# A residual block with Winograd convolutions: weight blocks in natural tap order, one transposing DMA each, ordered by a copy that writes at a distance

## The chip, the core and the metric

The kernel runs on one core of a Trainium2 chip. The metric is the device time of one execution in microseconds (us), the median of several runs. Besides the times there is one execution recorded by the profiler, with every instruction of every engine: TensorE (PE, with its weight loads as PEld), VectorE (DVE), ScalarE (ACT), GpSimd (POOL) and SyncE (SP), which here only issues DMAs.

## What is computed

A residual block of a diffusion model, on x of 2 x 512 x 64 x 64 in bf16. Two times in a row: a group norm over 4 groups, silu, and a 3x3 convolution from 512 to 512 channels; between them a time embedding is added per channel, at the end the input.

```python
def conv3(z, w):
    zp = jnp.pad(z, ((0, 0), (0, 0), (1, 1), (1, 1)))
    taps = [jnp.einsum("bchw,oc->bohw", zp[:, :, i:i+H, j:j+W], w[:, :, i, j]) for i in range(3) for j in range(3)]
    ...
h = conv3(_silu(gn(x, g1, be1)), w1)
emb = _silu(t_emb) @ w_emb
h = h + emb.reshape(B, C, 1, 1)
h = conv3(_silu(gn(h, g2, be2)), w2)
return x + h
```

## The kernel before, in words

**Tiling.** Channels are cut into 4 tiles of 128. An image is cut into 2 chunks of 32 rows, so each layer (convolution) has 4 chunks: 2 images by 2. For each chunk and each tile `ot` of output channels, `one_set` runs a set of matmuls over the 4 tiles `ct` of input channels. The rows are convolved by Winograd's method with outputs in fours: six positions of transformed inputs V (made by `make_v` on DVE and ACT from the silu in `a_tmp`) meet six positions of transformed weights U. Some chunks (chunk 2 of layer 0, all of layer 1) use it along the columns too for the two outer positions, with weights that `u_cols` combines once more.

**The weights.** The transformed weights of one `ot` and `ct` come from one block of 128 x 1152 elements: 128 output channels by 128 input channels by 9 taps, as they lie in DRAM with the tap running fastest. PE needs them with input channels on the partitions, so each tap must be turned (128 x 128). For layer 0, `ot` 0 and 1 (8 blocks), PE turns them (`transposes`, line 348). The other 24 blocks (layer 0, `ot` 2 and 3; all 16 of layer 1) are built with `by_dma`, in `u_blocks` (line 427):

1. SP loads the block into one of two `stage` buffers (`u_load`, line 420).
2. ACT copies it in two instructions into nine dense slots of U (`order`): the six outer taps (ky 0 and 2), then the three middle ones (ky 1). It reads with a step of 9 elements and writes densely (lines 442 and 444).
3. Two transposing DMAs are issued on SP (`turn`, line 331): 768 columns into slots 0 to 5 of U, 384 columns into the scratch `g1t`.
4. ACT writes a quarter of the three taps of ky 0 into U and a half of the middle taps into `g1t` (lines 447 and 448).
5. DVE makes the four inner positions by six additions for a pair of blocks (lines 479 to 484); in layer 1, `u_cols` adds three more (lines 408 to 410).

U has 22 slots of 128 columns per block: before, 0 to 5 hold the outer taps (two by two), 8 to 19 the inner positions, 6, 7, 20 and 21 column combinations. A block of layer 1 goes into the place of the block of layer 0 with the same `ot` and `ct`, once the last chunk of layer 0 has used that one; so the 16 blocks of layer 1 are built during the last chunk of layer 0 and the first sets of layer 1, while the 8 of layer 0 are built during the first chunk.

**What sets the order.** No engine's order is written by hand. Every operation is given to a planner (`_Plan`, line 23) with its engine, a cost in us, what it reads and writes. `issue` (line 132) plays the list through with these costs and emits the instructions in the order found; a wrong cost gives a worse order, not a wrong program. `act` (line 296) gives a copy from SBUF 0.00084 us per element plus 0.09, whatever its step. `turn` gives a transposing DMA 0.42 us of SP. Each engine then works through its queue in order and waits where an operand isn't ready; so ACT's copies for the weights stand in one queue with the evacuations of PE's accumulators (`m<-acc`, `w<-acc`), the silus (`a_tmp`) and the scaled rows for V (`src<-vt`). SP's queue holds loads, stores and the transposing DMAs.

Of the kernel before, what the change touches and what calls it, by code (L numbers as in the profile page):

```python
# [10 lines left out]
ALU = mybir.AluOpType  # L11
AX = mybir.AxisListType
F32 = mybir.dt.float32
BF16 = mybir.dt.bfloat16
# [145 lines left out]
def kernel(  # L160
# [13 lines left out]
    nc = tc.nc  # L174
    P = nc.NUM_PARTITIONS
# [7 lines left out]
    NKX = 3  # L183
# [11 lines left out]
    NSL = 22  # L195
# [18 lines left out]
    plan = _Plan()  # L214
# [4 lines left out]
    def view(t, off, dims):  # L219
        base = t[:] if not isinstance(t, bass.AP) else t  # L220
        return bass.AP(base.tensor, base.offset + off, [list(base.ap[0])] + [list(d) for d in dims])
# [34 lines left out]
    def size(a):  # L256
        n = 1
        for d in list(a.ap)[1:]:
            n *= d[1]
        return n  # L260
# [16 lines left out]
    def tt(out, in0, in1, op, **kw):  # L277
        plan.add("DVE", vcost("tt", (out, in0, in1)),
                 lambda: nc.vector.tensor_tensor(out=out, in0=in0, in1=in1, op=op), [in0, in1], [out], **kw)  # L279

    def ts(out, in_, c, op=ALU.mult, c2=None, op1=None, more=(), **kw):
        def emit():
            if op1 is None:
                nc.vector.tensor_scalar(out=out, in0=in_, scalar1=c, scalar2=None, op0=op)  # L284
            else:
                nc.vector.tensor_scalar(out=out, in0=in_, scalar1=c, scalar2=c2, op0=op, op1=op1)
        plan.add("DVE", vcost("ts", (out, in_)), emit, [in_] + list(more), [out], **kw)
# [8 lines left out]
    def act(out, in_, func=None, scale=1.0, bias=None, accum=None, **kw):  # L296
        fn = func or ACT.Copy
        ps = in_.tensor.name in psum
        c = size(in_) * (0.00093 if fn == ACT.Silu else 0.00081 if ps else 0.00084) + 0.09
        if accum is not None:  # L300
            c += 0.08

        def emit():
            extra = {}
            if bias is not None:
                extra["bias"] = bias
            if accum is not None:
                extra["accum_out"] = accum
            nc.scalar.activation(out=out, in_=in_, func=fn, scale=scale, **extra)  # L309
        reads = [in_] + [a for a in (scale, bias) if a is not None and not isinstance(a, float)]  # L310
        plan.add("ACT", c, emit, reads, [out] + ([] if accum is None else [accum]), **kw)
# [18 lines left out]

    def turn(out, in_):
        n = 256 * size(out)
        plan.add("SP", 0.42, lambda: nc.sync.dma_start_transpose(out=out, in_=in_), [in_], [out], nbytes=1.5 * n)

    def pool(emit, reads, writes, cost=0.45, **kw):
        plan.add("POOL", cost, emit, reads, writes, **kw)
# [11 lines left out]
    def transposes(bank, pairs, tokens, reads, cost):  # L348
        def emit():
            t = bank.get()  # L350
            for sel, in_ in pairs:
                nc.tensor.transpose(sel(t), in_, ident[:in_.shape[0], :in_.shape[0]])
        plan.add("PE", cost, emit, reads + [ident[:]], tokens, lead=TURN, lat=0.2, wait=WAIT)
# [47 lines left out]
    def slots(U, c0, n, first, dims):  # L401
        return view(U, ((c0 % 2) * NSL + first) * P, [[NSL * P, n]] + dims)

    def u_cols(layer, ot, c0, n, tmp):
        U = u_pair(layer, ot, c0)
        two = lambda first: slots(U, c0, n, first, [[1, 2 * P]])
        ck = view(tmp, 0, [[2 * NKX * P, n], [1, 2 * P]])
        tt(ck, two(0), two(4), ALU.add)
        tt(two(6), ck, two(2), ALU.subtract)
        tt(two(20), ck, two(2), ALU.add)  # L410

    def u_more(layer, ot, c0, n):
        U = u_pair(layer, ot, c0)
        g = lambda kx: slots(U, c0, n, 8 + 4 * kx, [[2 * P, 2], [1, P]])
        ck = view(g1t, 0, [[2 * P, n], [P, 2], [1, P]])
        tt(ck, g(0), g(2), ALU.add)
        tt(slots(U, c0, n, 2, [[P, 2], [1, P]]), ck, g(1), ALU.subtract)
        tt(g(1), g(1), ck, ALU.add)

    def u_load(layer, ot, ct, **kw):  # L420
# [6 lines left out]
    def u_blocks(layer, ot, c0, loads, tmp=None, dve=False, act_scale=True, by_dma=False):  # L427
        n = len(loads)
        tmp = g1t if tmp is None else tmp
        U = u_pair(layer, ot, c0)  # L430
        taps = [[P, NKX], [1, P]]
        for i, wn in enumerate(loads):
            ct = c0 + i
            Ut[layer][ot][ct] = U[:, ct % 2]
            one = lambda first, step: slots(U, ct, 1, first, [[step * P, NKX], [1, P]])
            raw = slots(U, ct, 1, 0, [[1, 6 * P]])
            mid = [view(tmp, (2 * i + h) * NKX * P, [[1, NKX * P]]) for h in range(2)]
            wv = wn[:].rearrange("p (c ky kx) -> p kx ky c", ky=3, kx=3)
            if by_dma:
                order = view(U, ((ct % 2) * NSL + 8) * P, [[1, 9 * P]])  # L440
                flat = view(U, (ct % 2) * NSL * P, [[1, 6 * P]])
                act(order[:, 0:6 * P].rearrange("p (kx j c) -> p kx j c", j=2, c=P),
                    wn[:].rearrange("p (c ky kx) -> p kx ky c", ky=3, kx=3)[:, :, 0:3:2, :])
                act(order[:, 6 * P:9 * P].rearrange("p (kx c) -> p kx c", c=P), wv[:, :, 1, :])
                turn(flat.rearrange("p (k o) -> p k o", o=P), order[:, 0:6 * P])
                turn(mid[0].rearrange("p (k o) -> p k o", o=P), order[:, 6 * P:9 * P])
                act(one(11, 4)[:, 0], flat.rearrange("p (kx j o) -> p kx j o", j=2, o=P)[:, :, 0, :], scale=0.25)
                act(mid[1], mid[0], scale=0.5)
                continue
            pa, pb = XBank("xa", [NKX, 2, P], BF16), XBank("xb", [NKX, P], BF16)  # L450
            transposes(pa, [((lambda t, kx=kx, j=j: t[:, kx, j, :]), wv[:, kx, 2 * j, :])
                            for kx in range(NKX) for j in range(2)], ["xa"], [wn[:]], 0.45)
            transposes(pb, [((lambda t, kx=kx: t[:, kx, :]), wv[:, kx, 1, :]) for kx in range(NKX)],
                       ["xb"], [wn[:]], 0.23)

            def copy(out, bank, tok, size_, sel=lambda t: t[:], scale=None):
                if dve:
                    plan.add("DVE", 0.075 + size_ * 0.00052,
                             lambda: nc.vector.tensor_copy(out=out, in_=sel(bank.get())), [tok], [out])
                elif scale is None:  # L460
                    plan.add("ACT", 0.07 + size_ * 0.0008,
                             lambda: nc.scalar.copy(out=out, in_=sel(bank.get())), [tok], [out])
                else:
                    plan.add("ACT", 0.07 + size_ * 0.0008, lambda: nc.scalar.activation(
                        out=out, in_=sel(bank.get()), func=ACT.Copy, scale=scale), [tok], [out])

            copy(raw.rearrange("p a (k o) -> p (a k) o", o=P).rearrange("p (kx j) o -> p kx j o", j=2),
                 pa, "xa", 2 * NKX * P)
            copy(mid[0].rearrange("p (k o) -> p k o", o=P), pb, "xb", NKX * P)
            if act_scale and not dve:  # L470
                copy(one(11, 4)[:, 0], pa, "xa", NKX * P, lambda t: t[:, :, 0, :], 0.25)
                copy(mid[1].rearrange("p (k o) -> p k o", o=P), pb, "xb", NKX * P, scale=0.5)
        g = lambda j: slots(U, c0, n, j, [[2 * P, NKX], [1, P]])
        up = lambda j: slots(U, c0, n, 8 + j, [[4 * P, NKX], [1, P]])
        m = lambda h: view(tmp, h * NKX * P, [[2 * NKX * P, n], [P, NKX], [1, P]])
        if dve or not act_scale:
            ts(up(3), g(0), 0.25)
            ts(m(1), m(0), 0.5)
        tt(up(1), g(0), g(1), ALU.add)
        tt(up(0), up(1), m(0), ALU.add)  # L480
        tt(up(1), up(1), m(0), ALU.subtract)
        tt(up(3), up(3), g(1), ALU.add)
        tt(up(2), up(3), m(1), ALU.add)
        tt(up(3), up(3), m(1), ALU.subtract)
        if layer == 1:
            u_cols(layer, ot, c0, n, tmp)

    def u_tap(U, pos, kx):
        if pos in (0, NPOS - 1):
            return U[:, 2 * kx + (1 if pos else 0), :]  # L490
        return U[:, 8 + 4 * kx + pos - 1, :]

    def u_col(U, j, c):
        return U[:, (0, 20, 6, 4)[c] + j, :]

    def u_col_more(U, j, c):
        return U[:, (8 + 2 * j, 12 + 2 * j, 2 + j, 16 + 2 * j)[c], :]

    more_buf = lambda ct: (a_tmp + src)[ct]

# [317 lines left out]
    for i, prm in enumerate((g1, be1, g2, be2)):  # L818
        o = gparm[CT * i:CT * (i + 1), :]
# [156 lines left out]
```

## Time and profile before

| what | value |
|---|---|
| median of 3 runs | 536.96 us (536.06 to 537.66) |
| the profiled execution | 537.9 us |
| its span, first to last instruction | 536.1 us |
| mean granted clock of PE | 0.986 |
| busy: PE, DVE, ACT, POOL | 493.1, 463.5, 362.7, 35.3 us |
| ordering copies of the 24 blocks on ACT | 38.6 + 21.4 us |
| scaled copies of the 24 blocks on ACT | 11.6 + 11.6 us |
| DVE's additions of 768 elements on U | 28.5 us with `g1t` (x52), 15.5 us without (x28) |
| transposing DMAs on SP | 48, median 2.9 us from issue to landing |

How to read the views: a group of instructions is named by line, engine, operation and tiles, out<-in, with partitions x elements and a count; behind the bar stand the busy time, the mean time of one in ns, and the idle time of the engine just before them with what ended most of it. Since all DVE and ACT operations go through a few helpers, one line number (279 for two-operand additions, 309 for ACT) covers many tiles, and the tile names tell them apart. A row of the waits gives the waiting engine and tile, the engine and tile waited for, the total in us, how many times and the longest. A row of the stretches gives start:end, its length, the busy time of PE, PEld, DVE, ACT and POOL with their instructions, PE's granted clock, the mean busy share of the 16 DMA engines and GB/s. The rows for one tile give shortest/median/longest duration in ns, then the first and last start. The slices cut the span into 40 parts of 13.4 us, each digit a busy share in tenths.

### The profile page before, as it was taken

Reading aid. Unit: us, or ns where it says so; the run is one execution under the profiler, and the core shown is the slowest. Engines: PE = TensorE matmul, PEld = TensorE weight load, DVE = VectorE, ACT = ScalarE, POOL = GpSimd, SP = SyncE. Lnnn points to the kernel's source line nnn. Section 1 sums busy time; section 2 is a strip of 40 time slices with the busy share of each in tenths; the row PEclk is TensorE's granted clock in tenths of the full one; section 3 lists DMA queues with packets and bytes.
Section 4 is the critical chain, followed back from the end, with each engine's and each line's share of the span. In section 5 each row is a group of like instructions: output and inputs, shape, how many; then the busy total and the mean of one; then the engine's idle time right before and its main releaser. Section 6 shows DMA issues by size and latency. Waiting matters only on the chain. (4 is left out here: it accounts for less than half of the span.)

```text
span 536.1 us, 7685 instructions
## 1 busy us (share of the span) xinstructions
PE 493.1 (92%) x2769; PEld 262.4 (49%) x2770; DVE 463.5 (86%) x1048; ACT 362.7 (68%) x412; POOL 35.3 (7%) x83
## 2 busy tenths in 40 slices
PE   3889968989999999999996979997999999999994
PEld 3544423434444555554442435553555555566762
DVE  3989677998999997698867879997799999999966
ACT  4788999999966785569998897252645645323332
POOL 1210000001100200000000000003010000000010
PEclk9999999999999999999998889998999999999999
DMA  8302965562112313127677462525245354333444
GB/s 308 118 23 67 187 139 124 181 261 83 28 54 81 95 67 118 40 79 162 187 154 159 122 172 44 137 88 136 62 119 160 82 158 120 78 80 79 96 101 117
DMA packets 46496, 62.56 MB, mean 117 GB/s; under 512 B 31099, under 2 KB 32251, under 8 KB 45691
## 3 DMA queue, kind: packets, MB, share of 16 engines
q1 hardware_dynamic: 44096, 53.95, 34.0%
q0 software_dynamic: 2160, 7.87, 8.9%
q8 instruction: 21, 0.34, 0.3%
q10 hardware_dynamic: 203, 0.27, 0.1%
q14 instruction: 16, 0.13, 0.1%
HBM read 38.22 MB, written 16.78 MB: 103 GB/s over the span
## 5 line engine op out<-in xcount | busy, mean ns | idle before, releaser
L591 PE MATMUL acc<-V,U 128*128 128x512 bf16 (+1 forms) x2368 | 461.1, 355 | 21.4 <-DVE U L279 7.5
L591 PEld LDWEIGHTS <-U 128*128 128x128 bf16 x2496 | 243.6, 98 | 242.4 <-issue 22.1
L279 DVE TENSOR_TENSOR V<-vt 128x1056 bf16<-128x1056 bf16 (+2 forms) x124 | 84.1, 696 | 5.1 <-PE acc L591 2.1
L309 ACT ACTIVATE w<-acc 128x1024 bf16<-128x1024 f32 (+1 forms) x33 | 32.7, 990 | 41.7 <-PE acc L591 33.3
L309 ACT ACTIVATE U<-stage 128x768 bf16<-128x768 bf16 (+1 forms) x48 | 58.4, 1268 | 3.2 <-PE acc L591 1.8
L309 ACT ACTIVATE m<-acc 128x1024 bf16<-128x1024 f32 x28 | 28.4, 1014 | 39.8 <-PE acc L591 31.1
L309 ACT ACTIVATE a_tmp<-src,nb,sc 128x2112 bf16<-128x2112 bf16 x20 | 42.8, 2144 | 14.9 <-DMA src<-h_scr 5.4
L309 ACT ACTIVATE src<-vt 128x528 bf16<-128x528 bf16 x54 | 34.3, 635 | 26.7 <-DVE vt L279 26.7
L279 DVE TENSOR_TENSOR w<-m,w 128x1024 bf16<-128x1024 bf16 (+1 forms) x66 | 44.2, 670 | 8.7 <-ACT w L309 7.8
L279 DVE TENSOR_TENSOR U<-U,g1t 128x768 bf16<-128x768 bf16 (+2 forms) x76 | 37.0, 498 | 7.7 <-DMA g1t<-U 6.3
L279 DVE TENSOR_TENSOR vt<-a_tmp 128x1056 bf16<-128x1056 bf16 x52 | 36.6, 704 | 7.4 <-ACT a_tmp L309 6.5
L309 ACT ACTIVATE src<-V 128x2048 bf16<-128x2048 bf16 x16 | 30.5, 1905 | 0.3
L309 ACT ACTIVATE y<-y 128x2048 bf16<-128x2048 bf16 x16 | 30.4, 1897 | 0.0
L279 DVE TENSOR_TENSOR U<-U 128x768 bf16<-128x768 bf16 (+1 forms) x36 | 18.3, 509 | 12.5 <-ACT U L309 4.5
L309 ACT ACTIVATE a_tmp<-V,nb,sc 128x2112 bf16<-128x2112 bf16 x12 | 25.7, 2146 | 1.9 <-DVE nb L292 1.9
L309 ACT ACTIVATE mb<-acc 128x1024 bf16<-128x1024 f32 x20 | 20.4, 1020 | 9.1 <-PE acc L591 6.2
L526 POOL MEMSET a_tmp<- 128x64 bf16 x32 | 6.5, 208 | 280.5 <-DVE vt L279 153.8
L327 POOL DMA_DIRECT2D y<-in_x_dram x15 | 13.2, 879 | 154.0 <-DVE y L279 119.8
L279 DVE TENSOR_TENSOR vt<-vt,a_tmp 128x1056 bf16<-128x1056 bf16 x32 | 22.6, 706 | 0.6
L279 DVE TENSOR_TENSOR y<-sd,acc 128x512 bf16<-128x512 bf16 (+1 forms) x34 | 21.9, 686 | 0.8 <-PE acc L591 0.6
L279 DVE TENSOR_TENSOR w<-w 128x1024 bf16<-128x1024 bf16 x31 | 21.4, 689 | 0.6
L292 DVE SCALAR_TENSOR_TENSOR y<-w 128x512 bf16<-128x512 bf16 x32 | 21.0, 689 | 0.5
(110 smaller groups left out, 378.4 us busy)
## 6 DMA issues: line engine op xcount, KB each, us to landing
stage<-in_w_dram SPq DMA_DIRECT2D x32, 288.0 KB, 2.9
src<-h_scr SPq DMA_DIRECT2D x16, 528.0 KB, 3.8
h_scr<-y SPq DMA_DIRECT2D x16, 512.0 KB, 2.6
y<-in_x_dram POOLq DMA_DIRECT2D x15, 512.0 KB, 5.6
out_dram<-y SPq DMA_DIRECT2D x15, 512.0 KB, 2.7
V<-in_x_dram SPq DMA_DIRECT2D x6, 1024.0 KB, 7.4
src<-in_x_dram SPq DMA_DIRECT2D x4, 528.0 KB, 4.7
V<-in_x_dram SPq DMA_DIRECT2D x4, 512.0 KB, 6.8
```

The source lines that it names most:

```text
L279: lambda: nc.vector.tensor_tensor(out=out, in0=in0, in1=in1, op=op), [in0, in1], [out], **kw)
L292: nc.vector.scalar_tensor_tensor(out=out, in0=in0, scalar=scalar, in1=in1, op0=op0, op1=op1, **extra)
L309: nc.scalar.activation(out=out, in_=in_, func=fn, scale=scale, **extra)
L327: q.dma_start(out=out, in_=in_, **extra)
L526: pool(lambda r=r: nc.gpsimd.memset(rows[:, r, 1:W + 1], 0.0), [], [rows[:, r, 1:W + 1]], cost=0.2)
L591: nc.tensor.matmul(ap, lhsT=l, rhs=r, start=k == 0, stop=k == total[key] - 1)
```

## The change

The nine taps of a block are now kept in their natural order, ky before kx, in the slots of U, so that all nine can be turned at once. For the 24 blocks built by DMA:

- one ACT copy of 1152 elements takes the place of two; it reads the stage densely, as it lies, and writes the nine taps of a channel 128 elements (256 bytes) apart, into slots 9 to 17;
- one transposing DMA of 1152 columns takes the place of two; it writes slots 0 to 8, so the middle taps land in slots 3 to 5 of U and no longer in `g1t`;
- the scaled copies read from the new places; the half of the middle taps still goes to `g1t`.

For all 32 blocks the inner positions move from slots 8 to 19 to slots 9 to 20; the sum of the two outer taps is kept in `g1t` (or its stand-in) instead of in U; the column combinations go to slots 3, 4, 5 and 21, and their operands lie in two runs of 128 columns instead of one of 256. The addresses that PE and the PE-turned blocks use follow. The planner counts 1.25 us of SP for a transposing DMA instead of 0.42, and gets a higher cost for ACT copies that read SBUF with a last step above 4 elements. The new ordering copy has a last read step of 1, so it is counted at 0.00084 us per element, 1.06 us.

```diff
@@ act, turn
+        if not ps and list(in_.ap)[-1][0] > 4:
+            c = size(in_) * 0.00187 + 0.1
...
-        plan.add("SP", 0.42, lambda: nc.sync.dma_start_transpose(out=out, in_=in_), [in_], [out], nbytes=1.5 * n)
+        plan.add("SP", 1.25, lambda: nc.sync.dma_start_transpose(out=out, in_=in_), [in_], [out], nbytes=1.5 * n)
@@ u_cols
-        two = lambda first: slots(U, c0, n, first, [[1, 2 * P]])
-        ck = view(tmp, 0, [[2 * NKX * P, n], [1, 2 * P]])
-        tt(ck, two(0), two(4), ALU.add)
-        tt(two(6), ck, two(2), ALU.subtract)
-        tt(two(20), ck, two(2), ALU.add)
+        two = lambda first, step: slots(U, c0, n, first, [[step * P, 2], [1, P]])
+        ck = view(tmp, 0, [[2 * NKX * P, n], [P, 2], [1, P]])
+        tt(ck, two(0, 6), two(2, 6), ALU.add)
+        tt(two(3, 1), ck, two(1, 6), ALU.subtract)
+        tt(two(5, 16), ck, two(1, 6), ALU.add)
@@ u_blocks
+            fl = lambda first, dims: view(U, ((ct % 2) * NSL + first) * P, dims + [[1, P]])
+            outer, mids = fl(0, [[6 * P, 2], [P, NKX]]), fl(3, [[P, NKX]])
+            up3, half_mid = fl(12, [[4 * P, NKX]]), view(tmp, (2 * i + 1) * NKX * P, [[P, NKX], [1, P]])
+            if by_dma:
+                order, taps9 = fl(9, [[P, 9]]), fl(0, [[P, 9]])
+                act(order.rearrange("p k c -> p c k"), wn[:].rearrange("p (c k) -> p c k", k=9))
+                turn(taps9, order.rearrange("p k c -> p (k c)"))
+                act(up3, fl(0, [[P, NKX]]), scale=0.25)
+                act(half_mid, mids, scale=0.5)
+                continue
-            if by_dma:
-                order = view(U, ((ct % 2) * NSL + 8) * P, [[1, 9 * P]])
-                flat = view(U, (ct % 2) * NSL * P, [[1, 6 * P]])
-                act(order[:, 0:6 * P].rearrange("p (kx j c) -> p kx j c", j=2, c=P),
-                    wn[:].rearrange("p (c ky kx) -> p kx ky c", ky=3, kx=3)[:, :, 0:3:2, :])
-                act(order[:, 6 * P:9 * P].rearrange("p (kx c) -> p kx c", c=P), wv[:, :, 1, :])
-                turn(flat.rearrange("p (k o) -> p k o", o=P), order[:, 0:6 * P])
-                turn(mid[0].rearrange("p (k o) -> p k o", o=P), order[:, 6 * P:9 * P])
-                act(one(11, 4)[:, 0], flat.rearrange("p (kx j o) -> p kx j o", j=2, o=P)[:, :, 0, :], scale=0.25)
-                act(mid[1], mid[0], scale=0.5)
-                continue
...
-        tt(up(1), g(0), g(1), ALU.add)
-        tt(up(0), up(1), m(0), ALU.add)
-        tt(up(1), up(1), m(0), ALU.subtract)
+        tt(t(0), g(0), g(1), ALU.add)
+        tt(up(0), t(0), mid, ALU.add)
+        tt(up(1), t(0), mid, ALU.subtract)
         tt(up(3), up(3), g(1), ALU.add)
-        tt(up(2), up(3), m(1), ALU.add)
-        tt(up(3), up(3), m(1), ALU.subtract)
+        tt(up(2), up(3), t(1), ALU.add)
+        tt(up(3), up(3), t(1), ALU.subtract)
@@ u_tap
-            return U[:, 2 * kx + (1 if pos else 0), :]
-        return U[:, 8 + 4 * kx + pos - 1, :]
+            return U[:, (6 if pos else 0) + kx, :]
+        return U[:, 9 + 4 * kx + pos - 1, :]
```

Left out here: the same renumbering in `u_more`, `u_col` and `u_col_more`, and the copies of the PE-turned blocks into the new slots.

More of the change, by code (lines that the diff above doesn't have):

```diff
@@ L405, in u_cols @@
         U = u_pair(layer, ot, c0)
-        two = lambda first: slots(U, c0, n, first, [[1, 2 * P]])
-        ck = view(tmp, 0, [[2 * NKX * P, n], [1, 2 * P]])
-        tt(ck, two(0), two(4), ALU.add)
-        tt(two(6), ck, two(2), ALU.subtract)
-        tt(two(20), ck, two(2), ALU.add)
+        two = lambda first, step: slots(U, c0, n, first, [[step * P, 2], [1, P]])
[3 more added lines that the diff above has]
+        tt(two(5, 16), ck, two(1, 6), ALU.add)
     def u_more(layer, ot, c0, n):
         U = u_pair(layer, ot, c0)
-        g = lambda kx: slots(U, c0, n, 8 + 4 * kx, [[2 * P, 2], [1, P]])
+        g = lambda kx: slots(U, c0, n, 9 + 4 * kx, [[2 * P, 2], [1, P]])
         ck = view(g1t, 0, [[2 * P, n], [P, 2], [1, P]])
         tt(ck, g(0), g(2), ALU.add)
-        tt(slots(U, c0, n, 2, [[P, 2], [1, P]]), ck, g(1), ALU.subtract)
+        tt(slots(U, c0, n, 1, [[6 * P, 2], [1, P]]), ck, g(1), ALU.subtract)
         tt(g(1), g(1), ck, ALU.add)
@@ L434, in u_blocks @@
             Ut[layer][ot][ct] = U[:, ct % 2]
-            one = lambda first, step: slots(U, ct, 1, first, [[step * P, NKX], [1, P]])
-            raw = slots(U, ct, 1, 0, [[1, 6 * P]])
-            mid = [view(tmp, (2 * i + h) * NKX * P, [[1, NKX * P]]) for h in range(2)]
-            wv = wn[:].rearrange("p (c ky kx) -> p kx ky c", ky=3, kx=3)
-            if by_dma:
-                order = view(U, ((ct % 2) * NSL + 8) * P, [[1, 9 * P]])
-                flat = view(U, (ct % 2) * NSL * P, [[1, 6 * P]])
-                act(order[:, 0:6 * P].rearrange("p (kx j c) -> p kx j c", j=2, c=P),
-                    wn[:].rearrange("p (c ky kx) -> p kx ky c", ky=3, kx=3)[:, :, 0:3:2, :])
-                act(order[:, 6 * P:9 * P].rearrange("p (kx c) -> p kx c", c=P), wv[:, :, 1, :])
-                turn(flat.rearrange("p (k o) -> p k o", o=P), order[:, 0:6 * P])
-                turn(mid[0].rearrange("p (k o) -> p k o", o=P), order[:, 6 * P:9 * P])
-                act(one(11, 4)[:, 0], flat.rearrange("p (kx j o) -> p kx j o", j=2, o=P)[:, :, 0, :], scale=0.25)
-                act(mid[1], mid[0], scale=0.5)
-                continue
@@ L450, in u_blocks @@
-            pa, pb = XBank("xa", [NKX, 2, P], BF16), XBank("xb", [NKX, P], BF16)
-            transposes(pa, [((lambda t, kx=kx, j=j: t[:, kx, j, :]), wv[:, kx, 2 * j, :])
-                            for kx in range(NKX) for j in range(2)], ["xa"], [wn[:]], 0.45)
+            fl = lambda first, dims: view(U, ((ct % 2) * NSL + first) * P, dims + [[1, P]])
+            outer, mids = fl(0, [[6 * P, 2], [P, NKX]]), fl(3, [[P, NKX]])
+            up3, half_mid = fl(12, [[4 * P, NKX]]), view(tmp, (2 * i + 1) * NKX * P, [[P, NKX], [1, P]])
@@ new lines, in u_blocks @@
+            if by_dma:
[5 more added lines that the diff above has]
+                continue
+            wv = wn[:].rearrange("p (c ky kx) -> p kx ky c", ky=3, kx=3)
+            pa, pb = XBank("xa", [2, NKX, P], BF16), XBank("xb", [NKX, P], BF16)
@@ L453, in u_blocks @@
+            transposes(pa, [((lambda t, kx=kx, j=j: t[:, j, kx, :]), wv[:, kx, 2 * j, :])
+                            for j in range(2) for kx in range(NKX)], ["xa"], [wn[:]], 0.45)
             transposes(pb, [((lambda t, kx=kx: t[:, kx, :]), wv[:, kx, 1, :]) for kx in range(NKX)],
@@ L465, in copy @@
                         out=out, in_=sel(bank.get()), func=ACT.Copy, scale=scale), [tok], [out])
-            copy(raw.rearrange("p a (k o) -> p (a k) o", o=P).rearrange("p (kx j) o -> p kx j o", j=2),
-                 pa, "xa", 2 * NKX * P)
-            copy(mid[0].rearrange("p (k o) -> p k o", o=P), pb, "xb", NKX * P)
+            copy(outer, pa, "xa", 2 * NKX * P)
+            copy(mids, pb, "xb", NKX * P)
             if act_scale and not dve:
[L471 to L475, printed above, removed]
+                copy(up3, pa, "xa", NKX * P, lambda t: t[:, 0], 0.25)
+                copy(half_mid, pb, "xb", NKX * P, scale=0.5)
+        g = lambda j: slots(U, c0, n, 6 * j, [[P, NKX], [1, P]])
+        up = lambda j: slots(U, c0, n, 9 + j, [[4 * P, NKX], [1, P]])
+        t = lambda h: view(tmp, h * NKX * P, [[2 * NKX * P, n], [P, NKX], [1, P]])
+        mid = slots(U, c0, n, 3, [[P, NKX], [1, P]])
         if dve or not act_scale:
             ts(up(3), g(0), 0.25)
-            ts(m(1), m(0), 0.5)
-        tt(up(1), g(0), g(1), ALU.add)
-        tt(up(0), up(1), m(0), ALU.add)
-        tt(up(1), up(1), m(0), ALU.subtract)
+            ts(t(1), mid, 0.5)
+        tt(t(0), g(0), g(1), ALU.add)
+        tt(up(0), t(0), mid, ALU.add)
+        tt(up(1), t(0), mid, ALU.subtract)
         tt(up(3), up(3), g(1), ALU.add)
-        tt(up(2), up(3), m(1), ALU.add)
-        tt(up(3), up(3), m(1), ALU.subtract)
+        tt(up(2), up(3), t(1), ALU.add)
+        tt(up(3), up(3), t(1), ALU.subtract)
         if layer == 1:
@@ L489, in u_tap @@
         if pos in (0, NPOS - 1):
-            return U[:, 2 * kx + (1 if pos else 0), :]
-        return U[:, 8 + 4 * kx + pos - 1, :]
+            return U[:, (6 if pos else 0) + kx, :]
+        return U[:, 9 + 4 * kx + pos - 1, :]
     def u_col(U, j, c):
-        return U[:, (0, 20, 6, 4)[c] + j, :]
+        return U[:, (6 * j, 5 + 16 * j, 3 + j, 6 * j + 2)[c], :]
     def u_col_more(U, j, c):
-        return U[:, (8 + 2 * j, 12 + 2 * j, 2 + j, 16 + 2 * j)[c], :]
+        return U[:, (9 + 2 * j, 13 + 2 * j, 1 + 6 * j, 17 + 2 * j)[c], :]
     more_buf = lambda ct: (a_tmp + src)[ct]
```

## The prediction

> **What bounds the kernel now.** I read the page's busy shares first, then its slices, then the busy time of each engine by stretch, then the waits inside the stretches that stand out.
>
> ```profile
> span 536.1 us, 7685 instructions
> ...
> PE 493.1 (92%) x2769; PEld 262.4 (49%) x2770; DVE 463.5 (86%) x1048; ACT 362.7 (68%) x412; POOL 35.3 (7%) x83
> ...
> PE   3889968989999999999996979997999999999994
> ...
> ACT  4788999999966785569998897252645645323332
> ...
> PEclk9999999999999999999998889998999999999999
> ```
>
> PE bounds the kernel over the whole span, and ACT at 68% looks harmless. The slices say otherwise: counted from 0, PE dips in slices 5, 6, 8, 21 and 23, and there ACT stands at 9 (8 in slice 21). In these places lie the 24 weight blocks that the change touches; only the dip in slice 27 has none. By stretch:
>
> ```profile
> core 0: us, PE busy (x) PEld busy (x) DVE busy (x) ACT busy (x) POOL busy (x), PEclk, DMA share, GB/s
> 52.00:93.00 41.00, 33.88 (x155) 14.36 (x154) 30.00 (x64) 40.50 (x50) 0.15 (x1) 1.00 0.67 147
> 93.00:130.00 37.00, 34.39 (x190) 15.70 (x189) 34.73 (x89) 35.97 (x41) 2.86 (x7) 1.00 0.51 181
> 247.00:335.00 88.00, 79.85 (x378) 38.03 (x377) 72.60 (x156) 78.61 (x95) 1.52 (x4) 0.94 0.62 143
> ```
>
> In the first row (8 of the 24 blocks) ACT works 40.5 of 41 us while PE idles 7.1; in the second PE idles 2.6; in the third (the other 16 blocks) 8.15. Between 130 and 240 PE idles 0.9 of 110 us, so there an easier ACT buys nothing. What can be won is thus 7.1 + 2.6 = 9.7 us and 8.2 us, plus a clock that falls after the later stalls. PE's waits, first in 52 to 93, then in 247 to 335:
>
> ```profile
> PE acc L591 <- DVE U L279: 7.1, 5, 2.6
> ```
>
> ```profile
> PE acc L591 <- DVE y L292: 5.2, 1, 5.2
> PE acc L591 <- ACT m L309: 3.0, 1, 3.0
> ```
>
> The names hide ACT. In order of time, the 5.2 us end at 292.81, when DVE had emptied an accumulator; DVE had stood 2.48 us at a U operation for the scaled middle taps, which ACT wrote at 290.76, behind 2.43 us of ordering copies at 285.07, a 1.90 us square and 1.57 us more of ordering copy. Ahead of the evacuation that ended the 3.0 us stall lie 4.74 us of ordering copies at 308.70 and another square. In the first stretch DVE waits for `U` of ACT 4.5 us.
>
> **The ordering copy, the main term.** Per block the old pair of copies reads with a step of 9 elements (18 bytes) and writes densely. Durations, kept apart by shape:
>
> ```profile
> L309 ACT ACTIVATE src<-V 128x2048 bf16<-128x2048 bf16 x16 | 30.5, 1905 | 0.3
> ...
> L309 ACT ACTIVATE U<-stage 128x768 bf16<-128x768 bf16 x24 | 38.6, 1624 | 3.2 <-PE acc L591 1.8 <-DMA stage<-in_w_dram 1.3
> ...
> L309 ACT ACTIVATE U<-stage 128x384 bf16<-128x384 bf16 x24 | 21.4, 913 | 0.0
> ...
> L309 ACT ACTIVATE U<-U 128x384 bf16<-128x384 bf16 x24 | 11.6, 514 | 2.6 <-DMA g1t<-U 2.6
> ```
>
> Dense both ways: (1905 - 514) / (2048 - 384) = 0.836 ns per element and 193 ns fixed. Read at a step: (1624 - 913) / 384 = 1.85 ns and 202 ns fixed. A block costs 1.624 + 0.913 = 2.54 us now. The new copy has 1152 elements, read densely and written 256 bytes apart. No ACT row writes that way, so I bound it:
> - lower end, the write is free: 0.193 + 1152 x 0.836 ns = 1.16 us;
> - the same engine's price for scattered reads: 0.202 + 1152 x 1.85 ns = 2.33 us;
> - upper end, from POOL's border memsets, the only scattered writes in the trace:
>
> ```profile
> L526 POOL MEMSET a_tmp<- x2: 188/248/307, 1.5 to 1.7; 128x64 bf16 x2
> ```
>
> ```profile
> L817 POOL MEMSET a_tmp<- x2: 283/336/388, 1.3 to 1.3; 128x68 bf16 x2
> ```
>
> The first fence is 64 dense elements, the second 68 scattered ones a moment earlier. Worst against best, (388 - 188) / 68 = 2.9 ns per element; best against worst, nothing. At 2.9 ns the copy costs 3.58 us.
>
> I take the lower end. Every scatter price in the trace that is beyond doubt is on the reading side (ACT's 1.85 ns; PE's weight loads from the stage, 143 ns against 98), and the new copy has no such read. The one pair of rows in which the write is scattered overlaps (283 against 307 ns) and so shows no sure price. This is a choice, not a measurement: ACT's scattered read is as near a row as a memset of another engine, and I keep both other cases below.
>
> [...]
>
> At 1.16 us a block saves 1.38 us of ACT: 11.0 us over 8 blocks, 22.1 us over 16.
>
> **The transposing DMAs.** 48 become 24; each holds SP for about 1.2 us whatever its width (medians 1.229 us for 768 columns, 1.210 us for 384), and both land in 2.9 us. I take 1.25 us of SP and 2.9 us to landing for 1152 columns; bounds 1.2 us and 2.9 + 1.2 = 4.1 us to landing. SP loses 24 x 1.2 = 29 us, but nothing waits for SP alone; stage loads, `src` loads and stores queued behind it start sooner. The outer taps come no later, though all 1152 elements must be ordered first (1.16 us, against 1.62 us for 768 now), and the middle taps sooner by about one DMA. Cost nothing; the DVE waits for DMA in 247 to 335 (4.7 for `g1t`, 4.1 for `U`) are the most it can add.
>
> **A wait that moves.** The middle taps now land in U, not in `g1t`, so the DMA no longer waits for DVE to finish with `g1t` (SP stood for it 10.9 us in 247 to 335, 3.4 in 52 to 93). The half-scaled copy on ACT now waits for it; behind it queue the evacuations that PE needs. Since 1.25 + 2.9 us of transposing come first, I cost it at nothing; its ends are nothing and those 14.3 us.
>
> **Edits with no cost.** The six DVE additions keep count and shape (554 ns, 768 elements), `t(0)` in `g1t` instead of in place. The column combinations have runs of 128 instead of 256; 512 elements take 420 ns and 768 in runs of 128 take 554 ns, 0.52 ns per element, so run length is not priced. The eight PE-turned blocks and PE's weight reads change addresses only. The planner's two new cost figures reorder the queues; only a spread of about 3 us either way can stand for that.
>
> **The sum,** against the profiled execution: 537.9 us, of which 1.8 lie outside its span; the median run is 0.9 below it.
> - 52 to 130: 11.0 us of ACT goes, PE's idle is 9.7 us. Late next are the 2.9 us landing, some 3.3 us of DVE (6 x 0.55) per pair, and V (PE waits 2.5 us for it near 100). I take half: 4.9.
> - 247 to 335: two stalls, 8.2 us, both behind a queue that loses 22.1 us. Two thirds: 5.5.
> - The clock is 0.89, 0.86 and 0.88 over 281 to 295, 295 to 308 and 308 to 322, with PE busy 8.83, 13.0 and 11.02 us: 0.11 x 8.83 + 0.14 x 13.0 + 0.12 x 11.02 = 4.1 us. It falls after the 5.2 us stall; half of it goes: 2.0.
>
> Together 12.4: 537.9 - 12.4 = 525.5, less 0.9 is **524.6 us**. All three in full, 22.0 us, would be 515; half the sum, 531. Own range 518 to 531.
>
> **Rivals.**
> - *The DMA engines bound the stretches next* (531 us): their share is 0.67 of 41 us and 0.62 of 88 us, so 27.5 and 54.6 us of busy time, below PE's own 33.9 and 79.9. That speaks against it; bursts and the moved wait for `g1t` speak for it. It would leave half the gain, 6.2 us.
> - *The scattered write costs what the scattered read cost* (533 us): 2.33 us per block saves 0.20, 1.6 us in the first stretch, 3.2 in the second of which half reaches PE, 1.6; one DMA less takes a third of DVE's DMA waits (8.8 + 1.6), of which half reaches PE, 1.7. Sum 4.9, less what reordering takes, some 4. For it: the one scattered ACT price in the trace. Own range 529 to 538. [...]
> - *The scattered write is dearer than both old copies* (552 us, the slower side). It decides from (2.54 - 0.19) us / 1152 = 2.04 ns per element, a tenth above the read's 1.85. At POOL's 2.9 ns each block adds 1.04 us: 8.3 us in the first stretch, where ACT has 0.5 us free, and 16.6 us in the second, of which 9.4 are free there, so 7.2. Sum 15.5. For it: all elements of a group of nine are 256 bytes apart, wider than any row here. Own range 538 to 560.
>
> **Chances.** Forecast 0.45, DMA bound 0.10, write as dear as read 0.25, dearer 0.20. A measurement of this kernel can tell about 0.3%, 1.6 us, from no change. Faster: 0.45 + 0.09 + 0.15 = 0.69. Within: 0.01 + 0.07 = 0.08. Slower: 0.03 + 0.20 = 0.23. The range 518 to 544 leaves out the forecast's fast tail and the dear half of the last case, under 0.2 together.
>
> **What would show it.** The ACT row `U<-stage` with 1152 elements: 1.16 us is right, 2.33 us the second rival, over 2.54 us the third. Then ACT's free time in the two stretches (0.5 and 9.4 us now), PE's idle there, the clock near 300, 24 transposes of about 1.25 us on SP, and no DVE wait for a DMA into `g1t`. The forecast is wrong if the copy is fast and PE still idles: then DMA landings or DVE's U operations are the chain.

## The result, and the profile after

The changed kernel takes **598.0 us** (median of 4 runs, 597.1 to 600.0), the kernel before 536.5. The ratio is 1.115, 95% interval 1.111 to 1.119: slower, where 524.6 us was forecast and 518 to 544 was the range. The page of the changed kernel (in it the helper line 309 has become 311, and 591 has become 589):

```profile
span 596.6 us, 7607 instructions
...
PE 508.1 (85%) x2769; PEld 267.7 (45%) x2770; DVE 461.8 (77%) x1048; ACT 428.8 (72%) x388; POOL 34.4 (6%) x83
...
PE   4887558599999999999655746698999999999995
...
ACT  3889999999975647789999999854265654523342
```

The span grows by 60.5 us. PE is idle for 88.5 us instead of 43.0, and its same matmuls take 15.0 us more. ACT has 66 us more work, and it all stands in one row, that of the ordering copy (columns as before):

```profile
L311 ACT ACTIVATE U<-stage 128x1152 bf16<-128x1152 bf16 x24 | 127.1, 5397 | 2.0 <-PE acc L589 2.0
```

5.40 us a copy, where the forecast had 1.16, the old pair takes 2.54 and the upper end of the bounds was 3.58. The loss lies in the stretches that were named: in the two rows below (8 blocks, then 15 of the other 16) ACT is busy 64 of 65 and 125 of 135 us, PE idles 25.7 and 40.2 us, and PE's clock is down to 0.81 and 0.85. Outside them PE idles 22.6 us, no more than before (27.7 us outside 52 to 93 and 247 to 335).

```profile
52.00:117.00 65.00, 39.34 (x160) 15.92 (x158) 33.31 (x71) 64.07 (x44) 0.31 (x2) 0.81 0.44 105
263.00:398.00 135.00, 94.82 (x405) 42.87 (x403) 78.97 (x173) 125.39 (x86) 1.52 (x4) 0.85 0.45 105
```

PE's waits now name ACT itself:

```profile
PE acc L589 <- ACT m L311: 36.2, 5, 11.3
PE acc L589 <- ACT w L311: 13.6, 3, 6.2
```

The longest of them in order of time (start, length, instruction):

```profile
302.34 5.35 ACT L311 ACTIVATE U<-stage 128x1152 bf16<-128x1152 bf16 x1
...
307.20 2.20 ACT L311 ACTIVATE y<-y 128x2048 bf16<-128x2048 bf16 x1
...
309.39 5.31 ACT L311 ACTIVATE U<-stage 128x1152 bf16<-128x1152 bf16 x1
...
314.92 2.13 ACT L311 ACTIVATE a_tmp<-src,nb,sc 128x2112 bf16<-128x2112 bf16 x1
...
317.37 1.00 ACT L311 ACTIVATE m<-acc 128x1024 bf16<-128x1024 f32 x1
...
318.41 1.01 PE L589 MATMUL acc<-V,U 128*128 128x512 bf16 x2 [11.33 <-ACT m L311]
```

PE stands 11.33 us, from 307.08 on, for one evacuation of 1.00 us, because ACT first does what is ahead of it in its queue: the last 0.6 us of one ordering copy, a square, a second ordering copy of 5.31 us, a silu (`a_tmp`) and two scaled copies that the rows leave out.

### The profile page after: what moved, and what is told of

Same layout as the page of the kernel before. It is cut to its first block, busy times and chain, and to the rows that moved or that the text cites. A ratio compares the mean times of both kernels' runs of the same rounds, so it can differ in the third digit from the quotient of the medians.

```text
span 596.6 us, 7607 instructions
## 1 busy us (share of the span) xinstructions
PE 508.1 (85%) x2769; PEld 267.7 (45%) x2770; DVE 461.8 (77%) x1048; ACT 428.8 (72%) x388; POOL 34.4 (6%) x83
## 4 chain that ended last, share of the span: by engine, by line
PE 39%; ACT 29%; DVE 18%; issue 9%; DMA 4%; POOL 0%; SPq 0%; ACTq 0%; DVEq 0%
PE acc L589 38%; ACT U L311 15%; ACT src L311 5%; DVE V L279 4%; DVE vt L279 3%; ACT a_tmp L311 2%; DVE w L279 2%; DVE y L292 2%; DVE U L279 1%; DVE y L279 1%; ACT g1t L311 1%; DMA U<-U 1%; ACT w L311 1%; ACT y L311 1%; ACT m L311 1%
## 5 line engine op out<-in xcount | busy, mean ns | idle before, releaser
L589 PE MATMUL acc<-V,U 128*128 128x512 bf16 (+1 forms) x2368 | 476.2, 363 | 65.7 <-ACT m L311 36.2
L589 PEld LDWEIGHTS <-U 128*128 128x128 bf16 x2496 | 248.1, 100 | 296.4 <-issue 82.3
L311 ACT ACTIVATE U<-stage 128x1152 bf16<-128x1152 bf16 x24 | 127.1, 5397 | 2.0 <-PE acc L589 2.0
L311 ACT ACTIVATE w<-acc 128x1024 bf16<-128x1024 f32 (+1 forms) x33 | 34.0, 1032 | 40.9 <-PE acc L589 40.8
L279 DVE TENSOR_TENSOR U<-U,g1t 128x768 bf16<-128x768 bf16 (+2 forms) x42 | 20.4, 488 | 21.5 <-ACT g1t L311 21.3
L279 DVE TENSOR_TENSOR U<-g1t,U 128x512 bf16<-128x512 bf16 (+2 forms) x74 | 32.5, 459 | 0.5
L279 DVE TENSOR_TENSOR g1t<-U 128x512 bf16<-128x512 bf16 (+2 forms) x41 | 18.6, 455 | 8.2 <-DMA U<-U 7.9
## 6 DMA issues: line engine op xcount, KB each, us to landing
src<-h_scr SPq DMA_DIRECT2D x16, 528.0 KB, 3.7
src<-in_x_dram SPq DMA_DIRECT2D x4, 528.0 KB, 5.1
```

The lines of the kernel that those rows point to most:

```text
L589: nc.tensor.matmul(ap, lhsT=l, rhs=r, start=k == 0, stop=k == total[key] - 1)
```

## The experiments

Three theories were tried: **W**, the write at a distance is the loss; **P**, the planner's wrong figure for it (1.06 us against 5.40) spoils the order of the queues; **L**, the new layout loses (one DMA, middle taps in U, the wait for `g1t` on ACT). Ratios are to the kernel before, with 95% intervals.

**The changed kernel, reading at a step and writing densely.**

```diff
-act(order.rearrange("p k c -> p c k"), wn[:].rearrange("p (c k) -> p c k", k=9))
+act(order, wn[:].rearrange("p (c k) -> p k c", k=9))
```

> The changed kernel, but its one ordering copy reads the stage with a step of 9 elements and writes densely; the planner counts it at 2.25 us. Theory W (the write at a distance is the whole loss): the copy takes 0.202 + 1152 x 1.85 ns = 2.33 us, the time falls from 598 us to 528 to 538, at or a little below the 536.5 of before, and the stalls of PE behind ACT shrink to those of before. Theory L (the new layout: one DMA, the wait for g1t moved to ACT, middle taps in U): the copy is 2.33 us all the same, but the time stays above 545. Theory P (the planner's wrong cost is most of it): 528 to 538 too, so this run does not tell P from W.

514.0 us, ratio 0.959 (0.955 to 0.963); the copy takes 2.353 us:

```profile
L311 ACT ACTIVATE U<-stage 128x1152 bf16<-128x1152 bf16 x24 | 56.0, 2353 | 2.5 <-PE acc L589 2.0 <-DMA stage<-in_w_dram 0.4
```

L falls: with this layout, and the new cost figures, the kernel is 23 us faster than before. It is also 14 us faster than W expected, so something else in the change gains. The kernel was run a second time as a neighbour of a later one:

> The version that reads at a step and writes densely once more, on the same chip as the pairs: 512 to 516, copies of 2.35 us. It is there so that a difference of under 1% to the pairs can be told.

514.3 us, ratio 0.957 (0.954 to 0.960).

**The write at a distance, its cost told to the planner.**

```diff
+if not ps and list(out.ap)[-1][0] > 4:
+    c = size(in_) * 0.00452 + 0.1
```

> The changed kernel, but the planner is told 5.3 us for the ordering copy instead of 1.06. Theory W: 24 x (5.40 - 2.54) = 69 us of ACT stay in the two stretches, and the time stays at 585 or above, with perhaps 5 to 12 us less from a better order. Theory P: the order was the loss, and the time falls below 565.

574.3 us, ratio 1.071 (1.067 to 1.075), copies of 5.51 us. Between W's 585 and P's 565: the wrong figure costs 24 us, and with the right one the write still costs 60 against the 514 of the first experiment.

**The write at a distance alone, in the kernel before.**

```diff
+taps = wn[:].rearrange("p (c ky kx) -> p c ky kx", ky=3, kx=3)
-act(..., wn[:].rearrange("p (c ky kx) -> p kx ky c", ky=3, kx=3)[:, :, 0:3:2, :])
-act(order[:, 6 * P:9 * P].rearrange("p (kx c) -> p kx c", c=P), wv[:, :, 1, :])
+act(order[:, 0:6 * P].rearrange("p (kx j c) -> p c j kx", j=2, c=P), taps[:, :, 0:3:2, :])
+act(order[:, 6 * P:9 * P].rearrange("p (kx c) -> p c kx", c=P), taps[:, :, 1, :])
```

> The kernel before, with its two DMAs and its layout, but its two ordering copies read the stage in runs of three and write at a distance (the outer taps 128 or 256 columns apart, the middle ones 128). Theory W: 768 and 384 elements at 4.5 ns take 3.7 and 1.9 us, 5.6 us a block against 2.54, and the time is 595 to 610. Theory L: the copies may be as dear, but the time stays under 570.

599.6 us, ratio 1.117 (1.112 to 1.123). The copies take 3.724 and 2.127 us, 5.85 a block. So the write at a distance, with a planner that does not know of it, gives a loss as large as the whole one without any other part of the change.

**The planner's figures alone, and the layout alone.** In the kernel before, the two cost lines of the change:

> The kernel before, with nothing changed but the planner's two cost figures of the change (0.00187 us per element for ACT copies that read at a step, 1.25 us of SP for a transposing DMA); its own copies then count 1.54 and 0.82 us instead of 0.74 and 0.41. If the 514 us of the changed kernel with the read at a step come from the better order alone, this run is at 515 to 522. If they come from the single copy and DMA and the freed g1t (ACT saves only 24 x 0.18 = 4.4 us), it stays at 532 to 537. In between, the two share the gain.

518.3 us, ratio 0.963 (0.957 to 0.969). One figure at a time:

> The kernel before with the planner's 1.25 us of SP for a transposing DMA and nothing else. If the DMA figure is what made the order of the 518 us run better, this is at 516 to 524; if the ACT figure is, at 532 to 538.

537.5 us, ratio 1.001 (0.998 to 1.004).

> The kernel before with the planner's 0.00187 us per element for ACT copies that read at a step and nothing else. The planner then knows of 24 x 1.2 = 29 us of ACT work that it did not count. If that made the order better, this is at 516 to 524; if the DMA figure did, at 532 to 538; 524 to 532 if both take part.

528.0 us, ratio 0.986 (0.980 to 0.991). The DMA figure does nothing by itself and some 10 us beside the ACT figure. The other way round, the first experiment's kernel with the old figures:

> The changed kernel with the copy that reads at a step and writes densely, but with the planner's old figures (0.00084 us per element, 0.42 us of SP). If the order is what gave the gain, this run is at 530 to 537; if the layout is, at 514 to 520.

532.2 us, ratio 0.990 (0.987 to 0.994). So the gain of the version at 514 is mostly a better order: the figures alone give 19 us, the layout alone 5.

**What a scattered write costs.** A kernel of copies only:

> No residual block at all: x goes to the output by one DMA, and ACT, DVE and POOL make copies of 1152 elements, four of each form, which differ in the step of the read or of the write. If each write into another 16-byte stretch has one fixed price, ACT's writes at steps of 8, 9, 16 and 32 elements all take near 5.4 us, like 9 places 128 apart, and steps of 2 and 4 take less. If the distance itself matters, steps of 8 to 32 stay near 1.2 to 2.5 us and 128 or 136 are dearer; if the 256 bytes fall on one bank, 136 is cheaper than 128. If the short inner run of nine is the price, the dense nest of nine takes over 4 us too. If the two bytes are the price, pairs of neighbours and 4-byte elements at 128 take about half as long or less per element. Reads 9 apart should take 2.33 us on ACT; a read 128 apart shows whether reads grow as well. DVE and POOL show whether the price is that of the engine or of the memory: as much as on ACT if it is the memory's.

All three engines pay for single elements 256 bytes apart (`far`), POOL as much as ACT (5.33 and 5.36 us, against 1.15 dense on both; DVE 2.92 against 0.46); `read` is the copy that reads 9 apart and writes densely. The row of DVE holds two distances (256 and 272 bytes, 2.73 to 3.03 us).

```profile
L44 ACT ACTIVATE ACT_far<-stage 128x1152 bf16<-128x1152 bf16 x8 | 42.4, 5357 | 0.0
L46 DVE COPY DVE_far<-stage 128x1152 bf16<-128x1152 bf16 x12 | 31.5, 2923 | 0.0
L48 POOL COPY POOL_far<-hold 128x1152 bf16<-128x1152 bf16 x4 | 21.3, 5332 | 0.0
L44 ACT ACTIVATE ACT_read<-stage 128x1152 bf16<-128x1152 bf16 x4 | 9.4, 2357 | 0.0
```

A dense nest of nine took 1.146 us, so the short inner run is not the price; 256 and 272 bytes took the same on ACT (5.31 to 5.64 us over both), so 256 bytes is not a bad distance of its own. The second probe gives every form a name:

> No residual block: x goes to the output by one DMA, and ACT makes copies of 1152 two-byte elements, four of each form, with names of their own. Dense writes 1.15 us, single elements 4 bytes apart 1.8, 8 bytes apart 2.6, 16, 18 and 32 bytes apart near 5.3 each, as the first probe suggests. Runs of 1, 2, 4 and 8 neighbours at a distance of 256 bytes, read densely: 5.3, 1.25, then 1.15 to 1.25 if a lone half of a 4-byte word is what is dear; 5.3, 2.7, 1.5, 1.2 if it is each stretch of 16 bytes once. Two neighbours that start on an odd element, thus in two words, near 5.3 a run or 2.7 an element-pair's share if words count, 1.25 if only neighbours count. The full ordering (reads 9 apart) with runs of 2, 4 and 8: 2.35, as with a dense write, if read and write overlap; up to 2.6 if they add.

The rows for each tile (shortest, median, longest in ns):

```profile
L35 ACT ACTIVATE w_at_four<-stage x4: 1461/1466/1467, 29.9 to 37.0; 128x1152 bf16<-128x1152 bf16 x4
```

```profile
L35 ACT ACTIVATE w_at_eight<-stage x4: 2722/3036/3037, 38.4 to 61.0; 128x1152 bf16<-128x1152 bf16 x4
```

```profile
L35 ACT ACTIVATE w_at_sixteen<-stage x4: 5336/5337/5337, 40.8 to 63.8; 128x1152 bf16<-128x1152 bf16 x4
```

```profile
L35 ACT ACTIVATE w_run_one<-stage x4: 5299/5302/5586, 108.0 to 126.8; 128x1152 bf16<-128x1152 bf16 x4
```

```profile
L35 ACT ACTIVATE w_run_two<-stage x4: 1461/1466/1469, 113.0 to 131.6; 128x1152 bf16<-128x1152 bf16 x4
```

```profile
L50 ACT ACTIVATE w_odd_two<-stage x4: 3394/3395/3396, 173.1 to 188.5; 128x1152 bf16<-128x1152 bf16 x4
```

```profile
L35 ACT ACTIVATE ordered_run_two<-stage x4: 1180/1180/1181, 141.4 to 150.8; 128x1152 bf16<-128x1152 bf16 x4
```

```profile
L35 ACT ACTIVATE ordered_dense<-stage x4: 2259/2259/2260, 156.1 to 169.0; 128x1152 bf16<-128x1152 bf16 x4
```

Lone elements 16, 18 and 32 bytes apart take 5.34, 5.48 and 5.29 us, and 256 bytes apart 5.30: over these distances the price stays within 4%. Pairs of neighbours at 256 bytes take 1.47 us, little over a quarter of 5.30 and far below its half, so it is the two-byte element written alone that is dear, not the long distance. Single 4-byte elements at 512 bytes took 2.27 us, (2.27 - 0.19) us / 1152 = 1.8 ns each (0.19 us is the fixed part of an ACT copy, worked out in the prediction from two dense shapes), as much as a scattered read at 1.85; a lone 2-byte one takes 4.4 ns. A pair that begins on an odd element takes 3.40 us, against 1.47 from an even one. Below 16 bytes the distance does matter (3.04 us at 8, 1.47 at 4), and the rows agree once the price is counted by stretch of 16 bytes: lone elements 4, 8 and 16 bytes apart put four, two and one into a stretch, and their time less 0.19 us, over 288, 576 and 1152 stretches, is 4.4, 4.9 and 4.5 ns. By this estimate, which rests on the distances of 4, 8 and 16 bytes alone, a stretch written in lone elements has one price of some 4.5 ns, whether one, two or four elements share it; a stretch written with one 4-byte element or one pair from an even element costs 1.8 to 2.2 ns, (2.27 - 0.19) us / 1152 and (1.47 - 0.19) us / 576. The surprise is the row `ordered_run_two`: the full ordering, two channels at a time, 1.18 us against 2.26 with a dense write. With runs of four or eight it takes 2.16 and 2.21 us. Two things stay open: why two alternating reads 18 bytes apart cost next to nothing (1.18 us against 1.14 dense) and four do not (2.16 us), and why the two probes differ on elements 4 bytes apart (1.79 to 1.82 us, then 1.47) and on pairs of neighbours (1.25 us, then 1.47).

**The ordering copy on POOL.** The same copy as `nc.gpsimd.tensor_copy`, counted at 2.4 us.

> The changed kernel, but the ordering copy is made by POOL, reading 9 elements apart and writing densely (2.30 us alone in the probe); POOL is busy 7% of the time. ACT loses another 24 x 2.35 = 56 us of work. If ACT still bounds the two stretches of the version at 514, the time falls to 505 to 511. If PE bounds them already (40.1 of 41 us busy in the first stretch), it stays at 511 to 516. If POOL's and DVE's accesses get in each other's way, the copies take over 3 us or DVE's additions grow, and the time rises above 517.

562.3 us, ratio 1.046 (1.039 to 1.054). ACT falls to 308 us of work, but DVE's busy time rises from the 460.6 us of the version at 514 to 508.7, and PE's longest waits are for DVE. The row of the copy, and two copies with DVE's additions of 768 elements beside them and after them in order of time:

```profile
L443 POOL COPY U<-stage 128x1152 bf16<-128x1152 bf16 x24 | 63.9, 2683 | 46.2 <-DMA stage<-in_w_dram 35.4 <-PE acc L591 10.8
...
55.47 2.40 POOL L443 COPY U<-stage 128x1152 bf16<-128x1152 bf16 x1 [0.15 <-DMA stage<-in_w_dram]
55.84 2.45 DVE L279 TENSOR_TENSOR U<-y,U 128x768 bf16<-128x768 bf16 x1
58.21 0.55 DVE L279 TENSOR_TENSOR U<-U 128x768 bf16<-128x768 bf16 x1
58.27 2.62 POOL L443 COPY U<-stage 128x1152 bf16<-128x1152 bf16 x1 [0.40 <-DMA stage<-in_w_dram]
...
58.86 2.44 DVE L279 TENSOR_TENSOR U<-U,y 128x768 bf16<-128x768 bf16 x1
61.23 0.55 DVE L279 TENSOR_TENSOR U<-y,U 128x768 bf16<-128x768 bf16 x1
```

The slowing is not spread over DVE's work. Exactly 24 of its operations, one beside each POOL copy and not only those on U, take 1.64 to 2.79 us and end 0.15 to 0.57 us after the copy, as if they began when it was done; the other additions of 768 elements stay at 0.55 us. The 24 make up some 46 of the 48 us that DVE gains in busy time. How much of the 48 us by which the kernel is slower than the version at 514 is that and how much the later loads (POOL waits 35.4 us for the stage) was not separated.

**Pairs at a distance: a version that beats both kernels.**

```diff
+act(order.rearrange("p k (c j) -> p c k j", j=2), wn[:].rearrange("p (c j k) -> p c k j", j=2, k=9))
```

> The changed kernel, but the ordering copy takes two channels at a time: it reads tap by tap two elements 9 apart and writes the two as neighbours, the pairs 256 bytes apart (1.18 us in the second probe); the planner counts it at 1.06 us. ACT loses 24 x (5.40 - 1.18) = 101 us of work against the changed kernel and 28 us against the version that reads at a step. If ACT still holds up the first stretch of that version (40.4 of 41 us busy), the time falls from 514 to 503 to 510. If PE and DVE bound it, it stays at 510 to 515. If the copy is slower among the other work than in the probe (over 2 us), 514 to 520.

**511.6 us**, ratio 0.952 (0.949 to 0.955), against 514.3 for the read at a step beside it. The copy takes 1.221 us. Its page, and the stretches of its weight blocks (8, then 16):

```profile
PE 486.1 (96%) x2769; PEld 260.8 (51%) x2770; DVE 460.0 (90%) x1048; ACT 333.5 (66%) x388; POOL 34.4 (7%) x83
...
PE   4789999999999999999999999999999999999994
```

```profile
52.00:93.00 41.00, 40.51 (x196) 17.51 (x195) 37.58 (x79) 37.70 (x50) 0.47 (x3) 1.00 0.77 197
...
222.00:325.00 103.00, 103.00 (x521) 50.70 (x520) 100.76 (x220) 78.54 (x98) 2.69 (x7) 1.00 0.62 153
```

PE has no dip left between start and end, and its clock stays at 1.00. ACT's further 26 us of freed work bring only 2.7 us, because PE bounds these stretches now.

## Why the prediction was wrong

**The failed step: "I take the lower end" for the ordering copy.** 1.16 us was taken, 5.40 us came. It failed in two ways. The reason for the choice (scatter prices stand on the reading side) was an absence of rows, and the write turned out 2.4 times as dear per element as the read, (5.40 - 0.19) / 1152 = 4.5 ns against 1.85. And the upper end was no bound: it came from two short memsets of 64 and 68 elements at the start, 2.9 ns at worst, while POOL's own copy of 1152 elements 256 bytes apart takes 5.33 us. With an end that could not be trusted, the range was too narrow on its slow side.

**The third rival was the right mechanism at too small a size.** (Its sum of 15.5 also leaves out the 0.5 us of free ACT time that it names; with it the sum is 15.0.) Its working with the measured copy: 8 x 2.86 - 0.5 = 22.4 and 16 x 2.86 - 9.4 = 36.4, so 537.9 + 58.8 = 596.7, and the profiled run took 598.4. The agreement is partly luck. In the order of the runs: 537.4 before; 518.3 with the two cost figures; 514.3 with the new layout as well; 574.3 with the write at a distance and its cost known; 598.0 as the change has it, with that cost counted at 1.06 us. So the rival leaves out a gain of 23 us and a loss of 24 us that cancel. Nor does its sum hold by parts: PE's idle time in the two stretches grew by 18.6 and 32.0 us (from 7.1 to 25.7 and from 8.2 to 40.2), less than 22.4 and 36.4, and the 15.0 us of slower matmuls, which it doesn't have, fill the gap.

**The planner: "only a spread of about 3 us either way" was wrong.** Its figures are worth 19 us (518.3 in place of 537.4), and the wrong one 24 us the other way. The trace of before held the hint: the planner counted 1.15 us for the two ordering copies of a block, and they took 2.54, so 33 us of ACT were unknown to it, in the very stretches where PE stood behind ACT.

**What bounds the kernel: right, and more is to be had.** With a copy of 1.22 us PE's idle time in both stretches goes and the clock is back at 1.00. The sum gave 524.6 for a copy of 1.16 us, and 515 with its three terms in full; the run gave 511.6. That doesn't show the shares "half", "two thirds" and "half" to be too low: the two cost figures alone give 19 of these 26 us, and no run has the fast copy with the old figures. One reading was not exact: the stretch from 247 to 335 holds 14 of the other 16 blocks, since the copies of the first two start at 238 to 243.

**The small terms held.** SP holds a wide transposing DMA for 1.32 us (1.25 taken), and it lands in 3.6 us (2.9 taken, 4.1 the upper end). ACT waits for DVE over `g1t` 0.5 us in all (nothing taken). DVE's additions of 768 elements stay at 0.55 us. The rival of the DMA engines falls: in the version at 511.6 their share is 0.77 and 0.62 in the two stretches, and PE is busy 40.5 of 41 and 103 of 103 us.

**The clock** was a term of 2.0 us; in the changed kernel the same matmuls take 15.0 us more, in stretches at 0.81 and 0.85. Those stretches hold stalls of PE of up to 9.7 and 11.3 us; in the version that reads at a step no stall after the start is over 2 us, and the clock is 1.00 in each of six stretches. How long a stall has to be for the clock to fall was not shown.

**The second rival, the write at the read's price, fell short too.** Its 2.33 us came from ACT's own reads 9 elements apart, and the copy that reads so does take 2.353 us; the write took 5.40. A short distance does not make a write of lone elements fast: 8 bytes apart they take 3.04 us against 1.14 dense, while pairs of neighbours 256 bytes apart take 1.47.

## What to carry to other kernels

A strided copy need not be cheapest on the side that looks free: before a scattered read is turned into a scattered write, time both; here two-byte elements that are written alone cost over twice a scattered read on ACT (4.5 ns against 1.85), and writing them in pairs took most of the price away (1.22 us a copy against 5.40). An operation that no trace shows has no upper bound from a few short instructions of another engine; then the range must say so, or the price must be measured first. Where a planner orders the queues, compare its figures with the trace: here two better figures took 19 us off the kernel before with no change to its work, and one that was 4.3 us too low, 24 times, cost 24 us.

## What the runs showed of the hardware

- Two-byte elements written alone, 16, 18, 32 and 256 bytes apart: 4.4 to 4.6 ns each on ACT (5.29 to 5.48 us for 1152, against 1.14 dense), 5.33 us for 1152 on POOL at 256 bytes, 2.73 to 3.03 us on DVE at 256 and 272 bytes. Pairs of neighbours from an even element at 256 bytes: 1.47 us for 1152 on ACT, 1.25 in the first probe. Single 4-byte elements at 512 bytes: 2.27 us for 1152.
- ACT reads 9 elements apart at 1.85 ns an element (2.35 us for 1152), but two such reads in turn, tap by tap, with pairs written, take 1.18 us for 1152 alone and 1.22 among other work, against 1.14 dense.
- POOL copies beside DVE: in each of the 24 cases one DVE operation took 1.64 to 2.79 us instead of 0.29 to 0.71 and ended 0.15 to 0.57 us after the copy; the copy itself took 2.50 us in the median, against 2.30 alone.
